# Splitting float64 weights into two float32 parts on VectorE alone, without GpSimd's two passes

## The chip, the cores and the metric

The kernel runs on one core of a Trainium2 chip. The metric is the device time of one execution in microseconds, the median of several runs.

## The reference

Three stages follow one another on 8 batches of 576 tokens. The feed-forward weights of the second stage come as float64, since the reference computes in float64 there.

```python
p_packed = sm_attn(p, k, v)            # 8 heads, 32 packed rows each
out = sm_attn(q, p_packed, p_packed)   # x: 4608 tokens x 512
h = x @ w_in                           # 512 x 2048
g = np.where(pos, h, np.where(neg, 0.0, (h + beta) ** 2 / (4.0 * beta)))
x = g @ w_out                          # 2048 x 512
expert_idx = np.argmax(x @ w_gate, axis=1)   # then per expert:
h = np.maximum(xe @ w1[e], 0.0); ye = h @ w2[e]; out = gate_w * ye
```

## The kernel before

All matrix products are made from operands in two parts (hi, rounded to the form TensorE takes, and lo, what the rounding left), with three matmuls each: hi*hi, hi*lo, lo*hi.

**The weights.** The two matrices of the first feed-forward come as 16 units of 1 MB, raw float64 words (tile `wr`, two int32 words per value: `low` and `high`). `load_unit` issues a unit's load on SyncE's queue. `prep_half(u, i)` turns one half of a unit (128 x 512 values, 32 halves in all) into hi and lo. ScalarE takes the absolute value of the high word (L282), VectorE clamps it (L283), shifts and masks it (L284) and puts the sign back (L285): `ca` is now a float32 with the leading bits of the value. ScalarE rounds `ca` into hi (L286). VectorE masks `ca`'s exponent out (L287, tile `pr`) and multiplies it by the low word (L288, written over `low` in `wr`). GpSimd subtracts hi from `ca` (L289) and adds the low word's part (L290); that is lo. Units with u % 4 < 2 go to tiles `ws` (first matrix; `spill` writes them to memory, L306), the others to `wo` (second matrix).

**The packing.** `packing()` loops over 16 groups (batch, four heads). `s1_load` loads keys and values (`kp`, `vr`; three buffers each), `s1_score` multiplies (`sc`, L387), `s1_exp` finds the maxima on VectorE (`nm`, L394 and L395) and takes the exponentials on ScalarE (L397), `s1_tr` transposes (`tp`, L405) and ScalarE copies (L408 to L410), `s1_av` multiplies by the values (`av`, L420). Into this loop 18 of the 32 halves are laid (units 0 to 8), the products of packed values and weights of the first pair of batches (`first_product`, `pp` L328, `pw` L331 and L332), the second attention of the first tile of tokens (`attn_chain`, tiles `s`, `qr`, `ah`, `al`, with GpSimd in L216, L225, L232), and the first three steps of the main loop.

**The main loop.** `step()` is one of 16 blocks of hidden values of one of 12 tiles of tokens: `ffn1` (`h`, L700), `hidden` (ScalarE L717, L718, VectorE L719 `rt`, ScalarE L732 `gh`, VectorE or GpSimd L733 `gl`), and `tile_y` of the step before (`y`, L705 to L707). The other 14 halves are laid into steps 3 to 9 by `prep_unit`. Behind the 12 tiles comes the routed feed-forward.

**The order.** SyncE's queue runs in the order of the program. On the other engines a list scheduler of the compiler sets the order before the run, from its own costs; at run time every engine works its list in order and waits on semaphores.

Of the kernel before, what the change touches and what calls it, by code (L numbers as in the profile page):

```python
# [12 lines left out]
I32 = mybir.dt.int32  # L13
# [10 lines left out]
P = 128  # L24
# [7 lines left out]
SL = 256  # L32
# [9 lines left out]
# High words of the float64 values 2**-127 and just under 2**128, read as float32.  # L42
# [4 lines left out]
# Tokens 256..319 of a pair's two batches make one block of 128; the first of the tiles with them  # L47
# keeps its half of the block's hidden values for the other.
# [4 lines left out]
def tile_kind(t):  # L53
    """How tile t cuts its pair of batches (576 tokens each): the first batch's first 320 (A), the
    second's last 320 (B), the 512 between (M)."""
    p, m = divmod(t, 3)
    return ("MAB", "ABM", "ABM", "MAB")[p][m]
# [10 lines left out]
def tile_pieces(t):  # L68
    """(first column, batch, first token, tokens) of the parts of tile t."""
    lo, hi = tile_start(t), tile_start(t) + tile_width(t)  # L70
    r = []
    for h in range(2):
        a, z = max(lo, S * h), min(hi, S * h + S)
        if a < z:
            r.append((a - lo, 2 * (t // 3) + h, a - S * h, z - a))
    return r


def tile_blocks(t):
    """First columns of the blocks of 128 finished in tile t; the common one's is COMMON."""  # L80
    k = tile_kind(t)
    if k == "A":
        cs = [0, P]
    elif k == "B":
        cs = [COMMON, HB, HB + P]
    else:
        cs = range(0, tile_width(t), P)
    return list(cs)
# [3 lines left out]
def attn_moe_kernel(ctx, tc, qT, kT, vv, pT, wcat, wg, w2cat, out):  # L92
# [17 lines left out]
    # ---- constants  # L110
# [11 lines left out]
    # the token in each row of each finished block  # L122
# [11 lines left out]
    # packed values, row (head of four, packed row); in odd batches the heads come as 2, 3, 0, 1  # L134
    packed = st2.tile([P, 2 * B, D], F32, name="packed")
    # one pair of batches' packed values for two heads 2k, 2k + 1, by dimension: the even batch's
    # columns, zeros, the odd one's (k even; swapped for k odd), then both without the zeros
    pk = st2.tile([P, 4, 2, 5 * D], F32R, name="pk")
    # the same in one part: the even batch's columns, then the odd one's (swapped for k odd)
    pkf = st2.tile([P, 4, 2 * D], F32, name="pkf")  # L140

    # ---- PSUM: 3 banks of outputs, 2 of hidden values and 3 for the rest; the packing of keys
    # and values borrows one of each of the latter
# [19 lines left out]
    # ---- helpers  # L163
# [5 lines left out]
    def build_pk(b, g):  # L169
        """The packed values of batch b for heads 4g..4g+3, by dimension."""  # L170
        ps = ps_tile(f"bt{b}_{g}")
        for h in range(2):
            pe.matmul(ps[D * h:D * h + D, :P], lhsT=packed[:, 2 * b + g, :], rhs=ident, start=True, stop=True)
        for s in range(2):
            k = 2 * g + (s ^ (b % 2))
            w = (3 - s) * D
            for h in range(2):
                r = slice(D * h, D * h + D)
                c = 2 * D * s + NP * h
                hi, lo = (pk[r, k, part, c:].rearrange("p (a c) -> p a c", c=NP)[:, 0:w // NP + 1:w // NP, :] for part in range(2))  # L180
                v = ps[r, D * s + NP * h:D * s + NP * h + NP].unsqueeze(1).to_broadcast([D, 2, NP])
                act.copy(hi, v)
                dve.tensor_tensor(out=lo, in0=v, in1=f32(hi), op=ALU.subtract)
                act.copy(pkf[r, k, D * s + NP * h:D * s + NP * h + NP], v[:, 0])
# [8 lines left out]
    def attn_chain(col0, b, ws, n, g, ah, al, pl, sfx):  # L193
        """Weights of the second attention for heads 4g..4g+3, tokens ws..ws+n of
        batch b, into columns col0.. of ah + al."""
# [3 lines left out]
        def load():  # L199
            qr = pl.tile([P, 2, SPLIT + HB], F32, name="qr" + sfx, tag="qr", bufs=2)  # L200
            act.dma_start(qr[:, :, :n], qT[b, 2 * g:2 * g + 2, :, ws:ws + n].rearrange("q p s -> p q s"))
            st["qr"] = qr
            # once the scores are there
            st["sT"], st["aT"] = qr[:, 0, :n].rearrange("p (a r) -> p a r", r=32), qr[:, 1, :n]
# [43 lines left out]
    def wtile(n, shape, dt, name):  # L248
        """A tile in weight place n."""
        return wpool.tile(shape, dt, name=name, tag=n)  # L250
# [5 lines left out]
    def load_unit(u):  # L256
        """Raw float64 words of two weight pieces: u = 4n, 4n + 1 are rows 256 (u % 4).. and
        columns 512 n.. of the first matrix, 4n + 2, 4n + 3 two chunks of rows of the second."""
        raw = RAW[u]
        if raw == "wr":  # L260
            raw = s1.tile([P, 2, 512, 2], I32, name=f"wr{u}", tag="wr", bufs=1)
        else:
            raw = wtile(raw, [P, 2, 512, 2], I32, f"wr{u}")
        sp.dma_start(raw.rearrange("p h a b -> p (h a b)"), wcat[u])
        wraw[u] = raw

    def prep_half(u, i):
        """Half i of unit u, float64, as two float32r parts."""
# [11 lines left out]
        ca = s1.tile([P, 512], I32, name=f"ca{u}_{i}", tag="ca", bufs=3)  # L280
        pr = s1.tile([P, 512], I32, name=f"pr_{u}_{i}", tag="prr", bufs=1)
# [3 lines left out]
        dve.scalar_tensor_tensor(out=ca, in0=high, scalar=-0x40000000, in1=ca, op0=ALU.bitwise_and, op1=ALU.bitwise_or)  # L285
        act.copy(hi, f32(ca))  # L286
        dve.tensor_scalar(out=pr, in0=ca, scalar1=-0x800000, scalar2=None, op0=ALU.bitwise_and)  # L287
        dve.scalar_tensor_tensor(out=f32(low), in0=low.bitcast(U32), scalar=2.0 ** -52, in1=f32(pr), op0=ALU.mult, op1=ALU.mult)  # L288
        pool.tensor_tensor(out=f32(ca), in0=f32(ca), in1=f32(hi), op=ALU.subtract)  # L289
        pool.tensor_tensor(out=lo, in0=f32(ca), in1=f32(low), op=ALU.add)  # L290
# [22 lines left out]
    # products: packed values of a pair of batches times their rows of the first matrix, columns  # L313
    # 512 n.. of it, as two parts; by batch, 32 rows to a head
# [3 lines left out]
    def first_product(n, g):  # L318
        """For the first pair, heads 4g..4g+3, while the engines that split the weights hold the
        time: more products, fewer copies."""  # L320
# [13 lines left out]
    def product(p, n, k):  # L334
        """For heads 2k, 2k + 1."""
# [12 lines left out]
    # ---- phase 1: packed keys and values of all batches  # L348
# [125 lines left out]
    # ---- phase 2: first feed-forward, second attention and gating  # L474
# [9 lines left out]
    def init_rows():  # L484
        """Rows of each expert's region that no token may fill: a token number out of range."""
# [6 lines left out]
    # by partition, tokens so far of each expert, each region's first row counted in  # L492
# [5 lines left out]
    def gate_items(t, j0, rows):  # L498
        """Work on the finished tokens of a tile, blocks j0 on of 128: expert, weight and row of each."""
# [60 lines left out]
    def index_tables(pl):  # L560
        """For rows p and p - 1 of a table: p; the whole slot meant; the offset into it; whether
        the row is a half slot's; and 1 more for the first triangle of ones, by expert."""
# [27 lines left out]
    def make_table(sums, used, nm):  # L590
        """Row s: expert and first row of slot s, whether the expert differs from slot s - 1's,
        and the number of half slots. Without `used`, the slots are the full ones so far, and
        the table comes with how many of the first EARLY each expert has; with it, the slots
        left: NMIN - EARLY of SL rows, then halves. An expert's tokens make slots of SL rows,
        and a half slot where at most HS are left over."""
# [43 lines left out]
        if used is not None:  # L639
# [4 lines left out]
            # whole slots beyond the table's, each two halves  # L644
# [8 lines left out]
            # number of halves  # L653
# [12 lines left out]
        if used is not None:  # L666
            # what is left over ends with the expert's last token
# [23 lines left out]
    def ffn1(t, fc, ps):  # L691
        """Hidden values before the activation."""
# [18 lines left out]
    def hidden(t, fc, ps):  # L711
        """The activation, as two parts; by finished block."""
# [40 lines left out]
    def evac_tile(t):  # L753
        rows = []
        for j, y in enumerate(y_tiles[t]):
            yr = work.tile([P, ROW], F32, name=f"yr{t}_{j}", tag="yr", bufs=4)
            # columns in the order (a, k, c) of 128 k + 32 a + c, for the slots' transposes
# [9 lines left out]
    def schedule_tile(t):  # L767
        base = FC * t
        p, m = divmod(t, 3)
        if m == 2 and t + 1 < NTILE:  # L770
            # the next pair of batches takes the places as the tiles are through with them
# [26 lines left out]
    # slots  # L798
# [42 lines left out]
    def lo_engine(sid, i, n):  # L841
        """The vector engine is busy with the gates of the last tile in the first slots."""
        return pool if sid < 2 or (sid == 2 and i == 1) else dve

    def split_w(sid, i, n):
        """Piece n of the first (i = 0) or second matrix: first[128 (n % 4) ..., 512 (n // 4) ...]
        or second[128 n ..., :], in a tile of two pieces."""
# [47 lines left out]
    def half_slot(sid):  # L895
        """A slot of HS rows: hidden values by rows first, then transposed."""
# [30 lines left out]
    # ---- main loop over the tiles of the first feed-forward  # L927
# [91 lines left out]
    # ---- phase 3: slots of the routed feed-forward  # L1019
# [33 lines left out]
def _layout(a):  # L1053
# [5 lines left out]
    # odd batches: heads 2, 3 before 0, 1 in each four  # L1059
# [38 lines left out]
```

## Time and profile before

| | |
|---|---|
| median of 3 runs | 1304.77 us (1304.32 to 1305.79) |
| span of the profiled execution, all that is recorded of its time | 1303.9 us |
| TensorE (PE) busy | 1209.4 us, 93% of the span |
| VectorE (DVE) busy | 984.9 us, 76% |
| ScalarE (ACT) busy | 757.2 us, 58% |
| GpSimd (POOL) busy | 514.5 us, 39% |

The span runs from the first to the last instruction of the profiled execution. A busy share over the whole span is a mean over stages with different limits: the weights are split in the first 213 us, and that stretch is read by itself. "Idle before" is the time an engine stood still ahead of an instruction, with the one that ended it; a releaser is inferred from semaphores.

### The profile page before, as it was taken

The page shows a single profiled execution, that of the slowest core. Times are in us where ns is not written, and L with a number is a line of the kernel's source. Part 1 is how long each engine was busy: PE and PEld are TensorE (multiplying, and loading weights), DVE is VectorE, ACT ScalarE, POOL GpSimd, SP SyncE. Part 2 cuts the span into 40 slices and gives each one's busy share as a digit, 9 for nine tenths or more (in the row PEclk, how much of TensorE's full clock was granted, in tenths as well). Part 3 has the DMA queues.
Part 4 walks back from the last instruction along what each step waited for, and adds up shares of the span by engine and source line. Part 5 has one row for each costly group of instructions (what it writes and reads, how often), then busy time and mean ns, then how long its engine had stood idle before and what let it go on. Part 6 is the DMA issues. An engine that isn't in the chain of part 4 may idle for free.

```text
span 1303.9 us, 22246 instructions
## 1 busy us (share of the span) xinstructions
PE 1209.4 (93%) x7234; PEld 1002.1 (77%) x7234; DVE 984.9 (76%) x2440; ACT 757.2 (58%) x1733; POOL 514.5 (39%) x746
## 2 busy tenths in 40 slices
PE   2687889999999999999999999898999999999997
PEld 1355667778777888778888887677899999999996
DVE  6788897998985877996859779788766566656653
ACT  3655555667666556666556465544565656565653
POOL 6564555742672113752021355778321212121120
PEclk9988999999999999999999999898999999999999
DMA  8877636024210232111132101500431111212150
GB/s 292 284 271 254 239 143 201 27 76 171 73 59 28 75 108 97 57 50 49 65 126 75 36 9 66 154 9 33 127 125 33 46 54 41 58 33 66 34 170 21
DMA packets 71340, 128.27 MB, mean 98 GB/s; under 512 B 10409, under 2 KB 46761, under 8 KB 69040
## 3 DMA queue, kind: packets, MB, share of 16 engines
q1 hardware_dynamic: 56528, 96.28, 22.4%
q0 software_dynamic: 5840, 18.95, 3.8%
q10 hardware_dynamic: 8848, 11.54, 2.9%
q8 instruction: 60, 0.98, 0.3%
q14 instruction: 64, 0.52, 0.1%
HBM read 162.31 MB, written 31.77 MB: 149 GB/s over the span
## 4 chain that ended last, share of the span: by engine, by line
PE 66%; DVE 15%; issue 3%; POOL 3%; ACT 1%; DMA 1%; ACTq 0%; SPq 0%; POOLq 0%; DVEq 0%
PE gh L870 15%; PE h L700 11%; PE y L705 8%; PE y L706 7%; PE y L707 7%; DVE jk L508 5%; PE gy L707 5%; PE gy L706 5%; PE gy L705 5%; PE pp L341 2%; DVE rt L719 1%; PE s L211 1%; DVE wr L288 1%; DVE ca L285 1%; POOL kept L733 1%
## 5 line engine op out<-in xcount | busy, mean ns | idle before, releaser
L700 PE MATMUL h<-ah,pw 128*128 128x256 f32 (+1 forms) x1024 | 245.4, 304 | 28.7 <-DVE rt L719 23.4
L870 PEld LDWEIGHTS gh<-gx,sw 128*128 128x128 f32 x1728 | 231.6, 193 | 14.3
L508 DVE CUSTOM_DVE_ANT_0 jk<-yr,wgb 128x512 bf16<-128x512 f32 x288 | 232.4, 807 | 9.8 <-ACT yr L758 7.8
L870 PE MATMUL gh<-gx,sw 128*128 128x256 f32 x1728 | 235.5, 285 | 0.0
L705 PE MATMUL y<-wo,gh 128*128 128x512 f32 x576 | 233.1, 405 | 2.1 <-ACT gh L732 1.2
L706 PE MATMUL y<-wo,gh 128*128 128x512 f32 x576 | 230.2, 400 | 0.0
L854 DVE TENSOR_TENSOR sw<-raw,sw 128x512 fp32r<-128x512 f32 x264 | 169.4, 693 | 74.9 <-ACT sw L853 74.9
L700 PEld LDWEIGHTS h<-ah,pw 128*128 128x128 f32 x1024 | 177.3, 191 | 55.8 <-DVE rt L719 33.7
L853 ACT CAST sw<-raw 128x512 fp32r<-128x512 f32 x304 | 169.3, 617 | 59.0 <-PE gy L707 55.4
L707 PE MATMUL y<-wo,gl 128*128 128x512 f32 x576 | 188.4, 400 | 2.0 <-POOL gl L733 1.2
L717 ACT ACTIVATE rt<-h,half 128x320 f32<-128x320 f32 (+1 forms) x192 | 111.1, 580 | 102.0 <-PE h L700 62.8
L700 PE MATMUL h<-al,pw 128*128 128x256 f32 (+1 forms) x512 | 153.2, 299 | 0.0
L732 ACT CAST gh<-rt 128x256 fp32r<-128x256 f32 (+2 forms) x256 | 100.4, 417 | 85.7 <-DVE rt L719 67.2
L719 DVE SCALAR_TENSOR_TENSOR rt<-h,rt 128x320 f32<-128x320 f32 (+1 forms) x192 | 105.3, 549 | 46.8 <-ACT rt L718 45.4
L838 POOL TENSOR_TENSOR gx<-xT,gx 128x1024 fp32r<-128x1024 f32 (+1 forms) x19 | 45.1, 2375 | 235.5 <-ACT gx L837 220.3
L705 PEld LDWEIGHTS y<-wo,gh 128*128 128x128 f32 x576 | 110.1, 191 | 26.5 <-ACT gh L732 3.8
L707 PEld LDWEIGHTS y<-wo,gl 128*128 128x128 f32 x576 | 105.4, 189 | 30.7 <-POOL gl L733 3.1
L706 PEld LDWEIGHTS y<-wo,gh 128*128 128x128 f32 x576 | 110.2, 191 | 19.0
L705 PE MATMUL gy<-sw,ggh 128*128 128x512 f32 x288 | 114.7, 398 | 0.0
L706 PE MATMUL gy<-sw,ggh 128*128 128x512 f32 x288 | 114.7, 398 | 0.0
L733 DVE TENSOR_TENSOR gl<-rt,gh 128x64 fp32r<-128x64 f32 (+1 forms) x192 | 97.1, 522 | 20.0 <-ACT gh L732 12.2
L874 ACT ACTIVATE ggh<-gh 128x256 fp32r<-128x256 f32 x144 | 55.0, 382 | 98.3 <-PE gh L870 93.7
(224 smaller groups left out, 1998.7 us busy)
## 6 DMA issues: line engine op xcount, KB each, us to landing
raw<-in_w2cat SPq DMA_DIRECT2D x76, 1024.0 KB
ws<-wsd SPq DMA_DIRECT2D x48, 512.0 KB
wr<-in_wcat SPq DMA_DIRECT2D x16, 1024.0 KB
kp<-in_kT SPq DMA_DIRECT2D x16, 576.0 KB
xb<-xs SPq DMA_DIRECT2D x72, 128.0 KB
vr<-in_vv SPq DMA_DIRECT2D x16, 512.0 KB
wsd<-ws SPq DMA_DIRECT2D x16, 512.0 KB
qr<-in_qT ACTq DMA_DIRECT2D x16, 320.0 KB
```

The lines of the kernel that those rows point to most:

```text
L508: dve.tensor_tensor_reduce(out=junk, in0=rows[j][:, :DM], in1=wgb[0][:, e, :], scale=1.0, scalar=0.0, op0=ALU.mult, op1=ALU.add, accum_out ...
L700: pe.matmul(ps[:, col0:col0 + n], lhsT=w[:, g, part, c], rhs=x[:, g, col0:col0 + n], start=(n_mm == 0), stop=(n_mm == 5))
L705: pe.matmul(y, lhsT=gh, rhs=wh, start=first, stop=False)
L706: pe.matmul(y, lhsT=gh, rhs=wl, start=False, stop=False)
L707: pe.matmul(y, lhsT=gl, rhs=wh, start=False, stop=last)
L717: act.activation(v[:, :W], ps[:, :W], AF.Relu, bias=half, scale=0.5)
L719: dve.scalar_tensor_tensor(out=v[:, :W], in0=ps[:, :W], scalar=1.0, in1=v[:, :W], op0=ALU.max, op1=ALU.min)
L732: act.copy(hi, v[:, c0:c1])
L733: lo_eng.tensor_tensor(out=lo, in0=v[:, c0:c1], in1=f32(hi), op=ALU.subtract)
L853: act.copy(w[:, 0, :], r)
L854: lo_engine(sid, i, n).tensor_tensor(out=w[:, 1, :], in0=r, in1=f32(w[:, 0, :]), op=ALU.subtract)
L870: pe.matmul(ps[:, :SL], lhsT=first(sid, 4 * (fc // 4) + k, part)[:, c], rhs=rh[:, k, :], start=(n_mm == 0), stop=(n_mm == 3 * KD - 1))
```

## The change

`prep_half` is rewritten behind L285. One more VectorE operation puts the upper three bits of the low word into the lowest bits of `ca` (shift right by 29, or), ScalarE rounds the whole word into hi, and one VectorE subtraction, `ca` less hi, is lo. The mask, the multiplication and the two GpSimd passes are gone, and tile `pr` with them; `ca` has four buffers instead of three. The rest of the diff takes comments out. Lines behind this place move up by two.

```diff
-        ca = s1.tile([P, 512], I32, name=f"ca{u}_{i}", tag="ca", bufs=3)
-        pr = s1.tile([P, 512], I32, name=f"pr_{u}_{i}", tag="prr", bufs=1)
+        ca = s1.tile([P, 512], I32, name=f"ca{u}_{i}", tag="ca", bufs=4)
+
         act.activation(f32(ca), f32(high), AF.Abs)
         dve.tensor_scalar(out=f32(ca), in0=f32(ca), scalar1=EXP_LO, scalar2=EXP_HI, op0=ALU.max, op1=ALU.min)
         dve.tensor_scalar(out=ca, in0=ca, scalar1=3, scalar2=0x3FFFFFFF, op0=ALU.logical_shift_left, op1=ALU.bitwise_and)
         dve.scalar_tensor_tensor(out=ca, in0=high, scalar=-0x40000000, in1=ca, op0=ALU.bitwise_and, op1=ALU.bitwise_or)
+        dve.scalar_tensor_tensor(out=ca, in0=low, scalar=29, in1=ca, op0=ALU.logical_shift_right, op1=ALU.bitwise_or)
         act.copy(hi, f32(ca))
-        dve.tensor_scalar(out=pr, in0=ca, scalar1=-0x800000, scalar2=None, op0=ALU.bitwise_and)
-        dve.scalar_tensor_tensor(out=f32(low), in0=low.bitcast(U32), scalar=2.0 ** -52, in1=f32(pr), op0=ALU.mult, op1=ALU.mult)
-        pool.tensor_tensor(out=f32(ca), in0=f32(ca), in1=f32(hi), op=ALU.subtract)
-        pool.tensor_tensor(out=lo, in0=f32(ca), in1=f32(low), op=ALU.add)
+        dve.tensor_tensor(out=lo, in0=f32(ca), in1=f32(hi), op=ALU.subtract)
```

The scheduler's lists change in their first 500 rows or so on each engine; behind these they are the same but for the numbers. Two places on VectorE matter here.

The first is the start, where the maxima of the second packing group (`nm`, from the scores `sc`) stand among the halves of units 0 to 2 (`ca`, `wr`, `ws`). Before:

```order
L285 SCALAR_TENSOR_TENSOR ca_1_442<-wr_177,ca_1_442 128x512
L287 TENSOR_SCALAR pr_1_443<-ca_1_442 128x512
L283 TENSOR_SCALAR ca_0_522<-ca_0_522 128x512
L183 TENSOR_TENSOR pk<-bt_0_342,pk 64x2x32
L288 SCALAR_TENSOR_TENSOR wr_177<-wr_177,pr_1_443 128x512
L394 TENSOR_REDUCE nm_241<-sc_236 128x1
L284 TENSOR_SCALAR ca_0_522<-ca_0_522 128x512
L183 TENSOR_TENSOR pk<-bt_0_342,pk 64x2x32
L395 TENSOR_SCALAR nm_241<-nm_241 128x1
```

And in the changed kernel:

```order
L286 SCALAR_TENSOR_TENSOR ca_1_433<-wr_177,ca_1_433 128x512
L183 TENSOR_TENSOR pk<-bt_0_336,pk 64x2x32
L284 TENSOR_SCALAR ca_0_510<-ca_0_510 128x512
L392 TENSOR_REDUCE nm_238<-sc_233 128x1
L284 TENSOR_SCALAR ca_1_591<-ca_1_591 128x512
L288 TENSOR_TENSOR ws_0_357<-ca_0_358,ws_0_357 128x512
L285 SCALAR_TENSOR_TENSOR ca_0_510<-wr_179,ca_0_510 128x512
L288 TENSOR_TENSOR ws_1_432<-ca_1_433,ws_1_432 128x512
L183 TENSOR_TENSOR pk<-bt_0_336,pk 64x2x32
L393 TENSOR_SCALAR nm_238<-nm_238 128x1
```

The maxima stay behind the first four halves: from the first L283 to them the list has 24 rows before (13 L283, L284 and L287, 8 L285 and L288, 3 L183) and 23 in the changed kernel (11 L283 and L284, 8 L285 and L286, 2 L288, 2 L183). Between them and their scaling, four large rows stand instead of one, two of them subtractions that wait for ScalarE.

The second place is one unit near the end of the packing loop, with the maxima (`nm`) and a step's activation (`rt`, from `h`) between its rows. Before:

```order
L285 SCALAR_TENSOR_TENSOR ca_0_1362<-wr_1043,ca_0_1362 128x512
L284 TENSOR_SCALAR ca_1_1374<-ca_1_1374 128x512
L287 TENSOR_SCALAR pr_0_1363<-ca_0_1362 128x512
L285 SCALAR_TENSOR_TENSOR ca_1_1374<-wr_1043,ca_1_1374 128x512
L288 SCALAR_TENSOR_TENSOR wr_1043<-wr_1043,pr_0_1363 128x512
L394 TENSOR_REDUCE nm_1267<-sc_1262 128x1
L287 TENSOR_SCALAR pr_1_1375<-ca_1_1374 128x512
L719 SCALAR_TENSOR_TENSOR rt_1555<-h_3_1540,rt_1555 128x512
```

And in the changed kernel:

```order
L285 SCALAR_TENSOR_TENSOR ca_0_1314<-wr_1007,ca_0_1314 128x512
L285 SCALAR_TENSOR_TENSOR ca_1_1323<-wr_1007,ca_1_1323 128x512
L392 TENSOR_REDUCE nm_1222<-sc_1217 128x1
L286 SCALAR_TENSOR_TENSOR ca_0_1314<-wr_1007,ca_0_1314 128x512
L286 SCALAR_TENSOR_TENSOR ca_1_1323<-wr_1007,ca_1_1323 128x512
L393 TENSOR_SCALAR nm_1222<-nm_1222 128x1
L717 SCALAR_TENSOR_TENSOR rt_1501<-h_3_1486,rt_1501 128x512
L288 TENSOR_TENSOR ws_0_1313<-ca_0_1314,ws_0_1313 128x512
L288 TENSOR_TENSOR ws_1_1322<-ca_1_1323,ws_1_1322 128x512
```

The halves of a unit now go side by side, and the two subtractions stand last, with other rows between them and the operation whose rounding they wait for.

## Rows read from the trace of the kernel before

**Rows 1.** Windows: stretch, us, then busy PE, PEld, DVE, ACT, POOL; PEclk, DMA share, GB/s.

```profile
12.00:40.00 28.00, 10.37 (x111) 5.81 (x112) 25.84 (x43) 13.04 (x34) 16.28 (x13) 1.00 0.63 215
40.00:132.00 92.00, 72.21 (x828) 47.40 (x831) 73.32 (x161) 54.80 (x150) 50.87 (x60) 0.89 0.83 292
132.00:213.00 81.00, 67.08 (x386) 51.49 (x375) 77.95 (x116) 43.38 (x79) 45.37 (x33) 0.96 0.56 192
213.00:1303.00 1090.00, 1057.58 (x5918) 896.50 (x5916) 804.89 (x2111) 644.38 (x1470) 392.80 (x568) 0.99 0.22 70
```

**Rows 2.** Timeline of DVE where POOL stands still: start us, us, instruction.

```profile
13.16 0.43 DVE L283 TENSOR_SCALAR ca<-ca 128x512 f32<-128x512 f32 x1 [0.21 <-ACT ca L282]
...
14.30 0.68 DVE L285 SCALAR_TENSOR_TENSOR ca<-wr,ca 128x512 int32<-128x512 int32 x1
14.90 0.42 DVE L284 TENSOR_SCALAR ca<-ca 128x512 int32<-128x512 int32 x1
15.24 0.42 DVE L287 TENSOR_SCALAR pr<-ca 128x512 int32<-128x512 int32 x1
...
109.48 0.68 DVE L733 TENSOR_TENSOR gl<-rt,gh 128x512 fp32r<-128x512 f32 x1
110.09 0.14 DVE L398 TENSOR_SCALAR rs<-rs 128x1 f32<-128x1 f32 x1
```

**Rows 3.** Timeline of DVE and POOL together, 15.8 to 18.2 us.

```profile
15.81 1.57 POOL L289 TENSOR_TENSOR ca<-ca,ws 128x512 f32<-128x512 f32 x1 [4.98 <-DVE pr L287]
...
16.18 1.75 DVE L288 SCALAR_TENSOR_TENSOR wr<-wr,pr 128x512 f32<-128x512 uint32 x1
...
18.07 1.34 POOL L290 TENSOR_TENSOR ws<-ca,wr 128x512 fp32r<-128x512 f32 x1 [0.68 <-POOL ca L289]
18.19 1.50 DVE L287 TENSOR_SCALAR pr<-ca 128x512 int32<-128x512 int32 x1
```

**Rows 4.** Windows, only instructions on tile ca: busy DVE, ACT, POOL.

```profile
12.00:40.00 28.00, 14.32 (x24) 7.57 (x12) 15.23 (x11) 1.00 0.63 215
40.00:132.00 92.00, 28.09 (x48) 15.04 (x24) 34.92 (x26) 0.89 0.83 292
132.00:213.00 81.00, 39.32 (x56) 17.53 (x28) 41.08 (x28) 0.96 0.56 192
```

**Rows 5.** Windows, only L288: busy DVE.

```profile
12.00:40.00 28.00, 9.22 (x6) 1.00 0.63 215
40.00:132.00 92.00, 14.44 (x12) 0.89 0.83 292
132.00:213.00 81.00, 16.10 (x14) 0.96 0.56 192
```

**Rows 6.** Timeline of the second packing group's scores, maxima and transposes.

```profile
18.79 2.19 PE L387 MATMUL sc<-kp 128*64 128x288 f32 x8 [0.91 <-DMA kp<-in_kT]
...
30.54 0.74 DVE L394 TENSOR_REDUCE nm<-sc 128x1 f32<-128x576 f32 x1
...
33.75 1.11 PE L405 MATMUL tp<-ident,kp 128*128 128x128 f32 x4 [12.77 <-ACT kp L397]
```

**Rows 7.** Waits of PE, 40 to 132 us: total us, times, longest.

```profile
PE h L700 <- DVE rt L719: 2.5, 2, 2.3
PE h L700 <- DVE nm L395: 2.2, 1, 2.2
PE av L407 <- DVE pw L332: 1.9, 2, 1.0
...
PE tp L405 <- DVE pw L332: 0.9, 1, 0.9
```

**Rows 8.** Waits of PE, 132 to 213 us.

```profile
PE h L700 <- DVE rt L719: 8.9, 5, 3.4
PE pp L328 <- POOL ws L290: 3.4, 2, 1.7
...
PE y L707 <- DVE gl L733: 0.3, 1, 0.3
```

## The prediction

> **What bounds the kernel now.** I read four stretches first, with the busy time of each engine in them [rows 1]. From 213 us to the end TensorE is busy in 1057.6 of 1090 us, 97%. That stretch sets its own pace, its order does not change, and it holds no weight splitting. What comes before it is different: TensorE is busy in 72.2 of 92 us from 40 to 132 us and in 67.1 of 81 us from 132 to 213 us, and its granted clock is a mean of 0.89 and 0.96 there. In the last of these stretches VectorE is the full engine: 77.95 of 81 us. So whatever lets the first 213 us end sooner moves everything behind them forward by the same amount, and VectorE is the place to look.
>
> Then I asked why VectorE is so full, and compared one operation with itself. Where GpSimd stands still, L283, L284 and L287 take 0.42 or 0.43 us, and the next one starts 0.34 us after L284; L285 takes 0.68 us and leaves 0.60 us; a subtraction of two tiles in SBUF (L733) leaves 0.61 us [rows 2]. Beside GpSimd's two passes the same kind of operation is three times as long: L288 1.75 us while L289 runs, L287 1.50 us while L290 runs, and they end 0.55 and 0.28 us behind GpSimd's pass [rows 3]. The reader should see that VectorE counts as busy in that time although it is held up. Its busy time therefore says too much, and GpSimd's passes cost twice: once on GpSimd, where they hardly matter, and once on VectorE.
>
> How much, stage by stage, comes from the time of the five prep operations (four on tile ca, and L288). Undisturbed, a half is 3 x 0.42 + 2 x 0.68 = 2.62 us. Measured [rows 4, 5]: 14.32 + 9.22 = 23.5 us for 6 halves before 40 us, where 15.7 would do (7.8 too many); 28.09 + 14.44 = 42.5 us for 12 halves from 40 to 132 us, where 31.4 would do (11.1 too many); 39.32 + 16.10 = 55.4 us for 14 halves from 132 to 213 us, where 36.7 would do (18.7 too many). Together VectorE loses 37.6 us beside 91.2 us of GpSimd's passes [rows 4].
>
> The Trainium skill (SBUF — State Buffer, Who interferes with whom) says that a VectorE instruction with two SBUF inputs, or one in a two-port mode, and a GpSimd instruction that reads SBUF exclude each other for a whole instruction, whichever starts first. The rows of the trace agree (1.75 and 1.50 us above). If by that rule each of the 64 passes held VectorE once for a whole pass of about 1.3 us, the loss would be 83 us; the rows give 37.6, and I go by the rows.
>
> **The change, part by part.**
>
> *VectorE's own work.* Removed per half: one L287 (0.34 us to the next start) and one L288 (0.60, as L285). Added: the shift-or of the low word, of L285's shape and types (0.60), and the subtraction (0.61). That is 0.27 us more per half: 1.6 us in the first stretch, 3.2 in the second, 3.8 in the third. The strided integer input of the shift-or is that of L285, so I see no other price. All of this lies on VectorE's path.
>
> *GpSimd's passes.* All 64 go. What stays on GpSimd before 213 us are the copies of packed rows and the passes of the attention; POOL is busy 112.5 us in the three stretches [rows 1], and 91.2 of these go [rows 4], so about 21 us of possible holding remain. The stalls counted above become small.
>
> *A new wait.* The subtraction stands in VectorE's queue behind ScalarE's rounding; before, GpSimd took that wait. Behind it are queued the maxima of the packing and the activations of the steps, for which TensorE waits. In the new order two other large rows lie between the shift-or and its subtraction, about 1.2 us, which covers one rounding of some 0.6 us if ScalarE is free. I take nothing for it in the sum, and up to 0.4 us a half in the range (13 us in all).
>
> *First stretch, before 40 us.* The scores of the second packing group are done at 18.79 + 2.19 = 21.0 us, but its maxima start only at 30.54 us, behind four halves of weights, and TensorE stands 12.77 us for the transposes behind them [rows 6]. VectorE's first weight operation starts at 13.16 us [rows 2]. The 24 rows ahead of the maxima need 13 x 0.34 + 8 x 0.60 + 3 x 0.2 = 9.8 us undisturbed and took 17.4. The 23 rows of the new order need 11 x 0.34 + 8 x 0.60 + 2 x 0.61 + 2 x 0.2 = 10.2 us: the maxima start at about 23.4 us, 7 us sooner. Their scaling has three more large rows in front of it than before, which takes some back. I take **6 us**; 4 if the subtractions wait for ScalarE, 9.5 at most (the scores are not there sooner).
>
> *Second stretch.* TensorE's waits that VectorE ended add up to 2.5 + 2.2 + 1.9 + 0.9 = 7.5 us [rows 7]. The loop here also hangs on loads (the DMA share is 0.83) and on SyncE's queue, whose order stays. VectorE gains 11.1 - 3.2 = 7.9 us net. Both figures are close; I take **7 us**, from 0 (loads and queue hold the pace) to 13 (7.9 and half of the 10 us that the clock of 0.89 costs in 92).
>
> *Third stretch.* VectorE's load falls from 77.95 by 18.7 - 3.8 = 14.9 to 63 us, under TensorE's 67.1 us: TensorE becomes the bound, and at most 81 - 67.1 = 13.9 us can go, 17 with the clock back at 1.0. The waits that VectorE or GpSimd's last pass ended are 8.9 + 3.4 + 0.3 = 12.6 us [rows 8]. I take **12 us**, down to 6 if half of these waits come back as waits for ScalarE.
>
> *The rest.* Raw tiles come free one GpSimd pass sooner, so the next loads can start sooner; I count nothing. A fourth buffer of ca takes the place of pr.
>
> The sum is 6 + 7 + 12 = 25 us. The profiled execution spans 1303.9 us, 0.9 under the median of the runs; 1304.8 - 25 gives **1280 us**.
>
> **Rivals.**
>
> 1. *Loads and ScalarE hold the first half.* The second stretch gives nothing, the third 6 to 12, the first 4 to 6: 10 to 18 us, 1287 to 1295. For it: the DMA share of 0.83, and the new wait in VectorE's queue. Against it: in the third stretch the share is 0.56 and ScalarE is busy 43 of 81 us.
> 2. *More than the waits.* TensorE also gets its clock back, and the second stretch gives 13, the third 17, the first 7 to 9: 37 to 39 us, 1265 to 1268.
> 3. *Slower: a full engine gets more work.* If the long operations are not due to GpSimd (but to the strided words, say), they stay long, and VectorE carries 0.27 us more in each of the 6 halves of the first and the 14 of the third stretch, where it sets the pace: 5.4 us, 1310 us. The same sign comes out of the new wait, if the subtraction stands more than 37.6 / 32 - 0.27 = 0.9 us on average. Against it: the same L287 takes 0.42 us with GpSimd still and 1.50 beside it [rows 2, 3]. The Trainium skill (Perfetto Trace Analysis, Optimizing Scalar/DVE Operations) speaks for the division of work of before: with VectorE saturated, handing some of its work to ScalarE or even GpSimd may make sense, though it adds that the shared port may undo that. By its first half the change is wrong; the rows show the second half at work.
> 4. *No change.* GpSimd's remaining passes hold VectorE just as much. They are 21 us where 112.5 were, so this leaves little room: within 3 us of 1304.8.
>
> **How the numbers follow.** The forecast, 1272 to 1288 us, gets 0.57. Rival 1 (1288 to 1300) gets 0.20, rival 2 (under 1272) 0.16, rival 3 0.04 and rival 4 0.03. A range of 1266 to 1294 us takes in the forecast and most of rivals 1 and 2; it leaves out the lowest of rival 2, the last third of rival 1, and rivals 3 and 4, some 0.15. A measurement of this kernel can tell about 0.2%, 2.6 us, from no change. Faster by more than that: 0.57 + 0.20 + 0.16 = 0.93; same 0.03; slower 0.04.
>
> **What would show it.** Right: L283, L284 and L285 have means close to 0.42 and 0.68 us, and no 1.5 us ones; the second group's maxima start near 23 us; in the stretch that ends with the last subtraction VectorE is busy about four fifths, not 96%, and TensorE's waits for L719 shrink; that subtraction ends near 190 us instead of a last GpSimd pass at 213 us; behind it the trace is the old one, shifted. Wrong: VectorE idle ahead of the subtraction for ScalarE, which would be the new wait; long operations without a GpSimd pass beside them, rival 3; or TensorE waiting for keys in the second stretch, rival 1. The prediction fails most easily in the second stretch, where I could not separate loads from VectorE.

## The result, and the profile after

The changed kernel takes **1284.8 us** (median of 4 runs, 1281.7 to 1285.5) against 1304.6 us before in the same comparison: a ratio of 0.984, with a 95% interval of 0.981 to 0.986. The profiled execution spans 1283.1 us, 20.8 less than before. The forecast was 1280 us, inside 1266 to 1294.

The page of the changed kernel gives the busy time of the engines:

```profile
PE 1206.7 (94%) x7234; PEld 999.4 (78%) x7234; DVE 947.2 (74%) x2440; ACT 755.5 (59%) x1733; POOL 422.2 (33%) x682
```

GpSimd loses 92.3 us of busy time, as 64 passes should. VectorE loses 37.7 us with as many instructions as before (2440), though by the prices of the prediction the new ones are 32 x 0.27 = 8.6 us more. So this is not less work, it is work that is no longer held, some 46 us of holding by this estimate.

To compare stretches, I cut both traces at the same amount of TensorE's work. By 40, 132 and 213 us the kernel before had started 119, 947 and 1317 matmuls. I take the start of the next one, the 120th, 948th and 1318th, as a mark (the expectations below name the marks by the count, 947th and 1317th). The changed kernel reaches the marks at 33.5, 128.3 and 192.2 us. Up to them both kernels have run the same kinds of matmuls, but for 10 of the 947 and 2 of the 1317. Windows from 0 (the count, give or take one, stands in brackets behind PE's time), then by stretch as in [rows 1]:

```profile
0.00:33.50 33.50, 12.94 (x120) 6.91 (x121) 21.31 (x55) 14.60 (x35) 11.78 (x78) 1.00 0.83 285
0.00:128.30 128.30, 88.08 (x948) 54.33 (x951) 86.48 (x218) 70.25 (x190) 25.39 (x110) 0.93 0.81 279
0.00:192.20 192.20, 148.66 (x1317) 102.47 (x1318) 145.09 (x334) 111.85 (x265) 32.81 (x118) 0.96 0.80 273
...
33.50:128.30 94.80, 75.14 (x830) 47.42 (x831) 65.17 (x164) 55.66 (x155) 13.61 (x32) 0.91 0.80 277
128.30:192.20 63.90, 60.58 (x384) 48.13 (x374) 58.61 (x117) 41.60 (x76) 7.42 (x8) 1.00 0.78 261
192.20:1283.00 1090.80, 1058.05 (x5918) 896.96 (x5916) 802.16 (x2106) 643.60 (x1469) 389.40 (x565) 0.99 0.21 69
```

The lead is 6.5 us after the first stretch, 3.7 after the second and 20.8 after the third. So the first stretch gave 6.5 us, the second took 2.8 back (94.8 us instead of 92), and the third gave 17.1 (63.9 instead of 81). The rest is the old trace, shifted: TensorE is busy 1058.05 of 1090.8 us, before 1057.58 of 1090.

The operations on `ca` and the subtraction answer to [rows 2] and [rows 3]. Columns: count, then shortest, median and longest in ns, then first and last start:

```profile
L283 DVE TENSOR_SCALAR ca<-ca x32: 407/419/429, 13.0 to 174.2; 128x512 f32<-128x512 f32 x32
L284 DVE TENSOR_SCALAR ca<-ca x32: 371/419/960, 13.4 to 176.3; 128x512 int32<-128x512 int32 x32
L285 DVE SCALAR_TENSOR_TENSOR ca<-wr,ca x32: 644/682/697, 14.1 to 178.4; 128x512 int32<-128x512 int32 x32
L286 DVE SCALAR_TENSOR_TENSOR ca<-wr,ca x32: 649/683/818, 15.0 to 180.6; 128x512 int32<-128x512 int32 x32
...
L288 DVE TENSOR_TENSOR ws<-ca,ws x16: 651/682/1078, 17.9 to 170.8; 128x512 fp32r<-128x512 f32 x16
...
L288 DVE TENSOR_TENSOR wo<-ca,wo x16: 642/681/702, 28.7 to 183.3; 128x512 fp32r<-128x512 f32 x16
```

Nothing here is longer than 1.08 us, and medians and shortest lie together; in the kernel before, beside the two passes, they took up to 1.80 us. The scores, maxima and transposes of the second packing group, as in [rows 6], from the timelines of TensorE and VectorE:

```profile
18.60 2.19 PE L385 MATMUL sc<-kp 128*64 128x288 f32 x8 [1.25 <-DVE ws L288]
...
23.43 0.76 DVE L392 TENSOR_REDUCE nm<-sc 128x1 f32<-128x576 f32 x1
...
27.79 1.11 PE L403 MATMUL tp<-ident,kp 128*128 128x128 f32 x4 [7.01 <-ACT kp L395]
```

The maxima start at 23.43 us instead of 30.54, and TensorE stands 7.01 us instead of 12.77. What TensorE waits for from 33.5 to 128.3 us, against [rows 7], and then from 128.3 to 192.2 us, against [rows 8]:

```profile
PE tp L403 <- ACT kp L395: 4.3, 5, 1.7
PE av L418 <- ACT vr L408: 3.6, 3, 2.4
PE s L211 <- DMA qr<-in_qT: 3.5, 1, 3.5
PE sc L385 <- DMA kp<-in_kT: 3.0, 1, 3.0
PE sc L385 <- ACT kp L395: 2.2, 2, 1.3
PE av L405 <- DVE pw L330: 0.8, 1, 0.8
...
PE h L698 <- DVE rt L717: 0.4, 1, 0.4
```

```profile
PE h L698 <- DVE rt L717: 2.5, 1, 2.5
PE pp L326 <- DVE pw L330: 0.5, 1, 0.5
PE h L698 <- ACT pw L329: 0.2, 1, 0.2
```

In the second stretch the waits that VectorE ended fell from 7.5 to 1.2 us, and waits for loads rose from 1.1 to 6.5. The largest part, waits for ScalarE's exponentials and copies, stayed: 12.1 us now, and 12.4 before. In all, TensorE waited 21.0 us in this stretch before and 20.2 after. The kernel before, 40 to 132 us, rows that [rows 7] doesn't have:

```profile
PE tp L405 <- ACT kp L397: 5.9, 5, 2.2
PE h L700 <- ACT pw L331: 2.7, 1, 2.7
...
PE sc L387 <- DMA kp<-in_kT: 1.1, 1, 1.1
```

In the third stretch the waits of 12.6 us fell to 3.0 that VectorE ends.

### The profile page after: what moved, and what is told of

It is laid out like the page before. It is cut to its first block, busy times and chain, and to the rows that moved or that the text cites. A ratio compares the mean times of both kernels' runs of the same rounds, so it can differ in the third digit from the quotient of the medians.

```text
span 1283.1 us, 22131 instructions
## 1 busy us (share of the span) xinstructions
PE 1206.7 (94%) x7234; PEld 999.4 (78%) x7234; DVE 947.2 (74%) x2440; ACT 755.5 (59%) x1733; POOL 422.2 (33%) x682
## 5 line engine op out<-in xcount | busy, mean ns | idle before, releaser
L506 DVE CUSTOM_DVE_ANT_0 jk<-yr,wgb 128x512 bf16<-128x512 f32 x288 | 232.0, 806 | 9.9 <-ACT yr L756 7.9
L851 ACT CAST sw<-raw 128x512 fp32r<-128x512 f32 x304 | 169.2, 617 | 59.7 <-PE gy L705 55.4
L731 DVE TENSOR_TENSOR gl<-rt,gh 128x64 fp32r<-128x64 f32 (+1 forms) x192 | 92.4, 497 | 23.0 <-ACT gh L730 15.2
```

The costliest lines, as they stand in the source:

```text
L506: dve.tensor_tensor_reduce(out=junk, in0=rows[j][:, :DM], in1=wgb[0][:, e, :], scale=1.0, scalar=0.0, op0=ALU.mult, op1=ALU.add, accum_out ...
L731: lo_eng.tensor_tensor(out=lo, in0=v[:, c0:c1], in1=f32(hi), op=ALU.subtract)
L851: act.copy(w[:, 0, :], r)
```

## The experiments

The theory: GpSimd's passes held VectorE, and lifting that made the gain, in the first and third stretches. The rivals: fewer dependent steps or a better list made it; or VectorE's room counts in the second stretch too. "The lead" is again by matmuls: how much sooner than in the kernel before a run reaches the three marks. Every ratio is to the kernel before on the same chip.

### GpSimd's passes put back, with nobody waiting for them

```diff
+        sc = s1.tile([P, 512], F32, name=f"scr{u}_{i}", tag="scr", bufs=1)
+        pool.tensor_tensor(out=sc, in0=f32(hi), in1=f32(hi), op=ALU.subtract)
+        pool.tensor_tensor(out=sc, in0=f32(hi), in1=f32(hi), op=ALU.add)
```

> The changed kernel with two GpSimd passes per half put back beside it: 128x512, both inputs the rounded half hi in SBUF, into a scratch tile of their own (which takes the place of the fourth buffer of ca). Nobody waits for their result, so the arithmetic, its waits and VectorE's own work stay those of the changed kernel. Theory (the gain came from GpSimd's passes no longer holding VectorE): VectorE's shift, mask and subtraction are long again beside the passes (1.3 to 1.7 us instead of 0.42 and 0.68), the maxima of the second packing group start near 30 us instead of 23.4, and most of the 20 us is gone: 1296 to 1308 us. Rival (the gain came from fewer dependent steps, or from a better order in the lists): VectorE's durations matter little and the time stays at 1283 to 1289 us.

Measured: 1305.2 us, ratio 0.9995 (0.998 to 1.001). The whole gain is gone, with the arithmetic, the waits and VectorE's instructions of the changed kernel. The lead is 2.2, 1.7 and 1.3 us, and the maxima of the second packing group start at 28.36 us, close to the 30 that were expected. The operations on `ca` and the subtraction in this run:

```profile
L283 DVE TENSOR_SCALAR ca<-ca x32: 411/419/1268, 13.3 to 197.1; 128x512 f32<-128x512 f32 x32
L284 DVE TENSOR_SCALAR ca<-ca x32: 408/420/1264, 13.8 to 199.6; 128x512 int32<-128x512 int32 x32
L285 DVE SCALAR_TENSOR_TENSOR ca<-wr,ca x32: 650/684/1528, 14.5 to 202.5; 128x512 int32<-128x512 int32 x32
...
L288 DVE TENSOR_TENSOR wo<-ca,wo x16: 679/1002/1524, 33.2 to 207.9; 128x512 fp32r<-128x512 f32 x16
```

The reader is to see the third number of each row: the longest is 0.85 to 0.88 us above the shortest, with GpSimd passes of 1.17 to 1.33 us on average beside. That the gain came from fewer steps is excluded. The passes also make GpSimd's other work wait behind them; the next run parts that from the holding.

### GpSimd just as busy, but only writing

```diff
+        pool.tensor_copy(sc[:, :1], f32(hi)[:, :1])
+        for m in range(5):
+            pool.memset(sc, float(m))
```

> As the run with two GpSimd passes beside, but GpSimd's work there only writes: per half one copy of a single column that waits for hi, then five fills of 128x512 of the scratch tile (0.53 us each by the profile of the kernel before, 2.6 us in all, as long as the two passes). Theory (VectorE is held by GpSimd's reading of SBUF, not by any work there): prep operations stay at 0.42 and 0.68 us, 1283 to 1290 us. Rival (any GpSimd instruction of this length holds VectorE): the prep operations are long again and the time is that of the run with the two passes, 1296 to 1308 us. Also possible: only one kind of the VectorE operations (the one-input shifts) is held.

Measured: 1284.2 us, ratio 0.985 (0.982 to 0.988): the gain stays, with GpSimd busy 525.8 us over the span, more than before the change (514.5). Timeline of VectorE in this run, then of GpSimd:

```profile
153.24 0.81 DVE L283 TENSOR_SCALAR ca<-ca 128x512 f32<-128x512 f32 x1
...
156.35 0.68 DVE L288 TENSOR_TENSOR wo<-ca,wo 128x512 fp32r<-128x512 f32 x1
156.95 1.28 DVE L285 SCALAR_TENSOR_TENSOR ca<-wr,ca 128x512 int32<-128x512 int32 x2
```

```profile
151.92 2.60 POOL L292 MEMSET scr<- 128x512 f32 x4
...
156.20 2.45 POOL L292 MEMSET scr<- 128x512 f32 x4
```

The subtraction and the shift-ors, with two inputs, run at full speed through four fills (0.68 us; 1.28 for two, one behind the other). The clamp, with one input, took 0.81 us instead of 0.42 beside a fill. So the kind of access decides, not GpSimd's being busy. The theory's number held; its third possibility, that one kind alone is held, shows too, but costs nothing that the time shows. The operations on `ca` and the subtraction are not all short in this run: the longest takes 1.53 us. All five of them over 0.85 us ran beside one of GpSimd's remaining passes that read (L216, L225, L232).

### The two passes on VectorE instead of GpSimd

The kernel before, with `pool` replaced by `dve` in L289 and L290.

> The kernel before with its arithmetic unchanged, but the two GpSimd passes of each half done on VectorE instead. Theory: the passes on GpSimd held VectorE 37.6 us in all, and on VectorE itself they cost 64 x 0.60 = 38.4 us, so the division of work was worth nothing: 1299 to 1309 us, with prep operations at 0.42 and 0.68 us. Rival (the long operations had another cause, such as the strided words): they stay long and VectorE carries 38 us more, of which 7 in the first and 17 in the third stretch are on the path: 1320 to 1330 us.

Measured: 1292.6 us, ratio 0.990 (0.987 to 0.992): neither range. The rival is excluded, and the theory's price for holding was too low: giving VectorE 64 operations more is 13 us *faster* than handing them to GpSimd (1305.6 us on that chip). The page says it in one row:

```profile
PE 1207.3 (94%) x7234; PEld 1001.8 (78%) x7234; DVE 979.0 (76%) x2504; ACT 757.2 (59%) x1733; POOL 424.7 (33%) x682
```

VectorE with 64 instructions more, 38.4 us of work, is busy 5.9 us less than the 984.9 of before, so some 44 us of holding went, not 37.6. The lead of 7.6, 6.5 and 12.7 us says where: the first stretch has all of its gain, the third some 6 us. Why the end moved more than VectorE's busy time was not parted further.

### One subtraction on GpSimd

In the changed kernel, `pool.tensor_tensor` for `dve.tensor_tensor` in L288.

> The changed kernel with its one subtraction per half on GpSimd instead of VectorE: 32 GpSimd passes of about 1.3 us instead of the 64 of before, and 32 x 0.61 = 19.5 us less work on VectorE. Theory (a GpSimd pass holds VectorE for about as long as the same work takes there, 37.6 / 64 = 0.59 us on average): nothing is gained, 1283 to 1295 us, with prep operations over 1 us again. Rival (VectorE is the full engine of the third stretch, so work taken off it pays): 1270 to 1279 us.

Measured: 1290.5 us, ratio 0.989 (0.986 to 0.991), as the theory had it, with operations on `ca` of up to 1.78 us again. Taking 19.5 us of work off the full engine made the kernel slower. The lead is 9.4 us at the second mark, more than the 3.7 of the changed kernel, and 16.0 at the third, so all of the loss lies in the third stretch:

```profile
122.60:197.00 74.40, 65.86 (x387) 51.76 (x376) 61.75 (x104) 41.07 (x75) 30.73 (x22) 0.93 0.75 255
```

VectorE, with 14 operations less there, is busy 61.75 us instead of 58.61, so it is held again. It is no longer full, though (61.75 of 74.4 us), and TensorE waits 1.8 us for the pass itself; how much of the loss is the holding and how much the longer way over GpSimd was not parted.

### Where VectorE is on the path: more work for it in one stretch alone

```diff
+        if 6 <= 2 * u + i < 18:        # and in the other run: 18 <= 2 * u + i < 32
+            sc = s1.tile([P, 512], F32, name=f"scr{u}_{i}", tag="scr", bufs=1)
+            for _ in range(2):
+                dve.tensor_tensor(out=sc, in0=f32(hi), in1=f32(hi), op=ALU.subtract)
```

The scratch tile needs the room of the fourth buffer of `ca`, so three buffers are the base of these runs:

> The changed kernel with three buffers for ca as before the change instead of four. It is also the base of the runs that need the room for a scratch tile. Theory: the buffers are no part of the gain, 1283 to 1288 us. Rival (the fourth buffer let the halves overlap and gave part of the gain): 1290 to 1298 us.

Measured: 1280.7 us, ratio 0.981 (0.979 to 0.983), its lead 7.1, 7.2 and 21.5 us. That is 2.3 us under the range of the theory, on the side away from the rival's: the fourth buffer is no part of the gain.

> The changed kernel (three buffers of ca, so that a scratch tile fits) with two subtractions more on VectorE in each of the 12 halves of units 3 to 8, into the scratch tile, for which nobody waits: 24 x 0.60 = 14.4 us of VectorE work in the second stretch alone. Theory (VectorE does not pace the second stretch, so the 8 us it gained there bought nothing): the time between the second and the sixteenth maxima stays at 97 to 103 us, and the kernel at 1280 to 1288 us. Rival (VectorE is on the path there): 105 us or more, 1288 to 1297 us.

> As the run with more VectorE work in the middle, but with the two subtractions more in the last 14 halves (units 9 to 15): 28 x 0.61 = 17 us of VectorE work in the third stretch alone. The base with three buffers of ca takes 1280.7 us and starts its 1317th matmul, the last that the kernel before had started by 213 us, at 191.5 us. Theory (VectorE is on the path in the third stretch, where the holding was lifted): that matmul starts 8 to 15 us later and the kernel takes 1288 to 1297 us. Rival (after the change TensorE is the bound there and VectorE has room): at most 4 us later, 1280 to 1285 us.

Measured: 1283.5 us (ratio 0.981, 0.979 to 0.984) with 14.4 us more in the middle, 1295.0 us (0.991, 0.989 to 0.993) with 17 us more at the end. Windows of the run with more in the middle, up to its third mark:

```profile
0.00:192.30 192.30, 148.87 (x1318) 104.59 (x1319) 158.33 (x355) 112.71 (x264) 34.29 (x116) 0.94 0.79 271
```

and of the run with more at the end:

```profile
0.00:202.20 202.20, 148.78 (x1317) 104.48 (x1318) 157.52 (x351) 111.58 (x263) 29.75 (x115) 0.93 0.74 255
```

VectorE is busy 158.33 and 157.52 us in these, the base 146.26 by its 191.5 us: nearly the same load in both, yet the first is 0.8 us late and the second 10.7. The room that the change gave VectorE in the second stretch bought nothing (at the second mark the first run is 2.5 us behind the base, which is within what two lists differ by, and catches up behind it); in the third it is worth most of what it is. Both theories held.

### What paces the second stretch

```diff
-                sp.dma_start(s["kr"], kT[b, 2 * g:2 * g + 2].rearrange("q p s -> p q s"))
+                sp.dma_start(s["kr"][:, :, :S // 2], kT[b, 2 * g:2 * g + 2, :, :S // 2].rearrange("q p s -> p q s"))
...
-            sp.dma_start(wsd[2 * n + g, q], f32(wstage[2 * n + g, q]))
+            pool.dma_start(wsd[2 * n + g, q], f32(wstage[2 * n + g, q]))
```

The first pair is the edit of the fewer bytes (in one run with all spills but the last left out as well), the second moves the spills to GpSimd's queue.

> The changed kernel with fewer bytes to move while the packing runs: of each group's keys only half is loaded (288 KB less of 576 KB, the other half of the tile stays zero), and of the eight units of the first matrix only the last is spilled, from which all later reloads are read. It leaves out part of the data, so its result is another. In the six kernels profiled so far the time from the second packing group's maxima to the sixteenth's is 97 to 102 us (before 100.6, changed 99.8, passes on VectorE 102.4), whatever VectorE did. Theory (loads pace the second stretch): with some 7 of 24 MB less there, that time falls to 75 to 92 us and the kernel to 1262 to 1277 us. Rival (the chain of scores, maxima, exponentials, transposes and copies paces it): 96 us or more, 1278 to 1287 us.

> The changed kernel with the spills issued from GpSimd's queue instead of SyncE's; the same bytes, in the same program order, but no longer ahead of loads in one queue. If SyncE's queue order paces the second stretch: the time between the second and the sixteenth maxima falls from 99.8 to 90 to 96 us, and the kernel takes 1274 to 1281 us. If the bytes pace it, or the chain between the engines: 97 to 102 us, 1281 to 1288 us.

> The changed kernel with half of each group's keys loaded and the spills as they were: 288 KB less in each of 16 groups, 3.7 MB of 24 in the second stretch, with SyncE's queue unchanged. It leaves out half of the keys. It parts the two edits of the run with fewer bytes, which started the 947th matmul (the last that the kernel before had started by 132 us) at 119.9 us, against 128.3 in the changed kernel and 124.8 with three buffers of ca. If the bytes pace the second stretch: 118 to 123 us. If the spills' place in SyncE's queue does (their move to GpSimd's queue alone gave 121.5 us): 125 to 129 us, the whole at 1280 to 1287 us.

> The changed kernel with the spills on GpSimd's queue and three buffers of ca, which gives the scheduler another list. If the gain of the moved spills (1278.8 us) is theirs: 1274 to 1280 us again. If it came from the order that the scheduler happened to find: 1281 to 1286 us.

> As the run before it, and the loads of units 3 to 15 go to GpSimd's queue too, so that SyncE's queue holds only keys and values from there on. If waits in SyncE's queue (68 us of it for the values' place in the second stretch) pace that stretch: the 947th matmul starts before 121 us, 1268 to 1276 us. If it was the spills alone: 1276 to 1282 us. If GpSimd's queue now stands for the units and holds up the copies of packed rows behind it: above 1284 us.

Measured, with the times of the second and the third mark:

| run | us | ratio (95%) | second mark | third mark |
|---|---|---|---|---|
| changed kernel | 1284.8 | 0.984 (0.981 to 0.986) | 128.3 | 192.2 |
| fewer bytes (keys and spills) | 1276.4 | 0.978 (0.976 to 0.980) | 119.9 | 185.9 |
| half the keys alone | 1262.6 | 0.968 (0.966 to 0.970) | 117.7 | 181.7 |
| spills on GpSimd's queue | 1278.8 | 0.979 (0.977 to 0.981) | 121.5 | 188.8 |
| the same, three buffers of ca | 1283.1 | 0.984 (0.982 to 0.987) | 130.7 | 190.4 |
| unit loads there too | 1280.0 | 0.981 (0.979 to 0.982) | 124.7 | 187.2 |

The whole time of the two runs with fewer bytes can't be compared: with other keys the tokens go to other experts, and from the last gating operation of the tiles (L506 in the changed kernel) to the end it takes 403.1 us in both instead of 411.2. The matmuls ahead of it can. With all bytes the second mark lies between 121.5 and 130.7 us in these runs, with half the keys at 117.7, 10.6 us sooner than in the changed kernel but only 3.8 sooner than with the spills moved. Windows from the first to the second mark: half the keys; keys and spills; spills on GpSimd's queue; and the run with the one subtraction on GpSimd, which moves all bytes too:

```profile
32.20:117.70 85.50, 69.58 (x831) 45.01 (x834) 64.50 (x163) 54.39 (x153) 15.56 (x32) 0.92 0.80 267
32.40:119.90 87.50, 69.50 (x828) 44.74 (x831) 62.77 (x163) 54.74 (x151) 14.86 (x32) 0.94 0.66 219
33.80:121.50 87.70, 68.71 (x827) 43.85 (x829) 66.32 (x168) 55.69 (x154) 19.64 (x38) 0.95 0.90 312
34.40:122.60 88.20, 72.34 (x829) 45.66 (x832) 61.05 (x152) 56.21 (x155) 30.96 (x44) 0.94 0.86 295
```

The changed kernel moved 277 GB/s in 94.8 us, 26.3 MB. Half the keys: 22.8 MB in 85.5 us. That alone looks as if the time went with the bytes, and 117.7 us lies just beside the 118 to 123 expected for that, where the chance that SyncE's queue does (125 to 129) fell. But the other rows speak against it: with the spills left out as well, 19.2 MB took 87.5 us, longer with fewer bytes, and with the spills moved 27.4 MB took 87.7. There is no one rate either, 219 to 312 GB/s. By the maxima it is the same: 91.6 us with half the keys, and 91.6 with the one subtraction on GpSimd, with all bytes; with keys and spills 75 to 92 were expected and 94.6 measured, a miss for the theory, and under the 96 of the rival too. So it is not shown that loads pace this stretch. The two runs with half the keys have its two shortest times, but by 0.2 and 2.2 us, less than two lists differ by.

The spills' queue is not shown as a cause either. Moving them gave 1278.8 us, in the range for it, but 97.3 us between the maxima, in the range against it; it was not repeated with three buffers (1283.1 us, expected 1274 to 1280), and with the unit loads moved as well it is 1280.0, in the range for the spills alone. What also differs between those is the list that the scheduler finds.

Two things stand in the rows all the same. ScalarE ended more of TensorE's waits in this stretch than any other, in all 14 versions. And SyncE's queue stands for the place of the values, which `av` has to free, 46.7 to 58.5 us of the stretch in nine versions; in the changed kernel:

```profile
SPq L376 <- PE av L418: 57.3, 11, 10.8
```

So the loads wait for TensorE in their turn, and their bytes need not be what is late. More buffers for the values, or fewer exponentials, were not tried. What paces this stretch stays open.

No version came out that is clearly better than the others with all bytes. The fastest, spills on GpSimd's queue at 1278.8 us, lies below the changed kernel's interval, but its edit alone doesn't explain it.

## Why the prediction was right

*The cause.* Right, and shown: two passes that read put the whole 20 us back, fills of the same length don't. The Trainium skill (SBUF — State Buffer, Who interferes with whom) says that a two-input VectorE instruction excludes GpSimd's reads but not mere writes, and that a two-port one excludes both; the run with fills agrees with it in the first part (0.68 us beside fills) and, for the clamp at 0.81 us, fits the second, though no run shows which mode the clamp was in.

*VectorE's own work*, 0.27 us more per half: the added shift-or has a median of 683 ns, that of L285 682.

*GpSimd's remaining passes* (rival 4): little; the longest operations beside them are the 0.96, 0.82 and 1.08 us above.

*The new wait*: near enough the nothing that it was taken at. VectorE's waits from 12 to 192 us hold one row for ScalarE's rounding:

```profile
DVE wo L288 <- ACT wo L287: 1.0, 1, 1.0
```

*First stretch*, 6 us: 6.5 by matmuls. The maxima were forecast at 23.4 us and started at 23.43.

*Second stretch*, 7 us: **the step that failed**. It gave nothing, -2.8 us by matmuls (+0.9 by the maxima, which start 7.1 us sooner in the second group and 8.0 in the sixteenth). The waits of [rows 7] were counted as time that goes, and VectorE did end them: they fell from 7.5 to 1.2 us. But others ended as late. Waits for loads rose by 5.4 us, and the 12.4 us of waits for ScalarE, which the forecast did not weigh, stayed; in all 21.0 us became 20.2. 14.4 us of further VectorE work there cost nothing that shows. This is the outcome of rival 1 for this stretch, and the end of the range named for it, 0. Its cause, loads and ScalarE, fits the waits; which of them it is stays open.

*Third stretch*, 12 us: **mis-sized**, it gave 17.1, about the bound that was named for the case that the clock comes back. The granted clock there is 1.00 instead of 0.96, but TensorE's busy time fell from 67.08 to 60.58 us, where the clock alone makes it 64.4; the rest was not parted. VectorE's load fell to 58.61 us, not to 63, since the forecast took the holding off the five prep operations alone. L733, 12 operations in this stretch, had been held too (busy VectorE and GpSimd on that line, before, then after, where it is L731):

```profile
132.00:213.00 81.00, 11.36 (x12) 0.00 (x0) 0.96 0.56 192
128.30:192.20 63.90, 8.05 (x12) 0.00 (x0) 1.00 0.78 261
```

The errors of the second and the third stretch cancel in part: the sum of 25 us measured 20.8. That the whole came out so near 1280 us is to that extent luck.

*VectorE's share there.* Wrong: about four fifths were forecast up to the last subtraction, but VectorE is full from 140 to 180 us:

```profile
128.30:184.00 55.70, 52.38 (x337) 40.91 (x327) 53.30 (x105) 37.72 (x69) 3.94 (x4) 1.00 0.73 260
140.00:180.00 40.00, 36.68 (x187) 28.50 (x186) 40.00 (x78) 27.04 (x47) 2.89 (x3) 1.00 0.62 226
```

The last subtraction ends at 184.0 us, not 190. TensorE did not become the only bound: both engines are nearly full, and 17 us more for VectorE still cost 10.7. The stretch shrank with VectorE's work, so its share stayed.

## What to carry to other kernels

An operation that takes three times its own shortest time may be held by another engine: compare like with like before believing a busy share, and look at what runs beside it. Work handed to GpSimd need not be free for VectorE: here both read SBUF, and 64 passes on GpSimd cost more than the same 64 on VectorE itself. A wait that a faster engine ends is only gained where nothing else is due right behind it: add work to that engine in that stretch alone, and see whether anyone notices.

## What the runs showed of the hardware

GpSimd fills beside VectorE did not slow two-input operations, but held some one-input ones (0.42 us for 512 columns). Counted in the trace of that run, of the 44 two-input prep operations that ran beside fills alone none took over 0.15 us more than the shortest of its kind; of the 17 one-input ones 6 did, by up to 0.46 us. Beside passes that read, both kinds were held, by up to 0.9 us in the run with the passes put back.

The list that the scheduler finds counts: two versions with the spills on GpSimd's queue that differ only in a buffer of `ca`, and through it in the list, reach the second mark at 121.5 and 130.7 us, and end at 1278.8 and 1283.1. Differences of that size between versions of this kernel can't be laid to an edit without a second list. That holds for the second stretch, 85.5 to 98.1 us in the 14 versions. The third parts clearly: 59.7 to 67.8 us in the nine versions with neither reading passes for the weights on GpSimd nor more work for VectorE there, 74.4 to 81.4 in the five others. So the gain in the third stretch is not an accident of one list.
